# Two block transposes of a staged Fourier mixing, moved from VectorE to DMAs through DRAM

## The chip, the cores and the metric

The kernel runs on one core of one Trainium2 chip. The metric is the device time in microseconds. Where a time comes from the profile, it is from one profiled execution, and its span runs from the first to the last instruction.

## What is computed

The input x has 8 batches of 3008 rows with 256 columns. Along the rows a real Fourier transform is taken, multiplied by a complex filter, and transformed back; the result, 24,064 rows of 256, goes through a two-layer network with a leaky ReLU.

```python
X = np.fft.rfft(x, axis=1)
F = (filt_r + 1j * filt_i)[None, :, :]
y = np.fft.irfft(X * F, n=x.shape[1], axis=1)
h = y.reshape(24064, 256) @ w_in        # 256 x 2048
out = np.maximum(0.01 * h, h) @ w_out   # 2048 x 256
```

## The kernel before

**The transform.** 3008 is split as 94 x 32, so that each direction is two stages of small matrix products with a transpose between them. For one batch the steps are these:

- *s1* (`s1_group`, 16 groups, matmul on L175): a 94-point transform of two of the 32 residues n, with the n-th slices of `x_sb` as moving data. The result has 128 partitions: four quadrants of 32 (real and imaginary parts of two sets of 24 frequencies k, the rest padding). A copy from PSUM writes it to the buffer `big[(4b) % 3]` (`spread`, L185).
- *t1* (`t1_part`, four parts, L197): VectorE transposes 32 x 32 blocks, which exchanges k on the partitions with n along the row, in each quadrant. It goes from one `big` buffer to the next.
- *s2* (`s2_group`, 12 groups, L215): the 32-point transform with the twiddle factors, two frequencies k a group, each with its own weights in `f2_sb`. VectorE then multiplies by the filters into `p1` and `p2` (L220 to L222), and GpSimd adds them to `y` (L224).
- *sa* (`sa_group`, 12 groups, L231): the inverse 32-point transform of y, copied by ACT to a `big` buffer, again by `spread`.
- *t2* (`t2_part`, four parts, L205): the second block transpose.
- *sb* (`sb_group`, 16 groups, L243): the inverse 94-point transform, whose weights are slices of the transposed data; VectorE copies the result to `yt` (L246), which holds two batches.

Batch 0 goes through other functions (`first_s1` to `first_sb`) before the network starts; it uses `t1_part` too, and `first_t2`. In what follows "b" is batches 1 to 7.

**The network.** It runs in 47 chunks of 512 rows. A chunk has 8 slots. In a slot `moe1_group` does a part of the first layer (four matmuls of 512 columns, L380, and an activation on ACT to `gt`, L385), and `moe2_slice` a part of the second layer of the chunk before (eight matmuls of 256 columns, L394). Every second slot ends with a copy to an output staging buffer `ost` on ACT (L401), and every fourth with a store to DRAM on SyncE (L405). There are six staging buffers.

**What sets the order.** All work is written in a fixed order (`tc.manual_schedule()`). The table `tasks` says which transform groups stand in which slot; `plan` fills it. In a slot come first the network's first part, then the transform groups in the order in which they were entered, then the second part:

```python
if ci < NCHUNK:
    moe1_group(ci, g)
for f in tasks.get(slot, ()):
    f()
if ci > 0:
    moe2_slice(ci - 1, g)
```

Batch b has to be in `yt` by slot 47b. With z = 47(b-1) - 8 for b from 2 on, s1 takes two groups a slot from z, t1 stands at z+9 to z+12, s2 from z+13 with a step of 1.25 slots (`(step * g) // 4` with step 5), sa three slots after its s2, t2 at z+32 to z+35 and sb, two groups a slot, from z+37. Batch 1 has the same stages in slots 0 to 39, with one s2 group a slot. The s1 copies of batch 1 go three times in four to VectorE, all others to ACT.

**The x load.** `x_sb` holds one batch. In the slot of the last s1 group of batch b, `x_load(b + 1)` (L136) is put on GpSimd's queue; it converts from float32 and waits for the last matmul that reads `x_sb`. GpSimd also flips a sign in `fb_sb` once (L362), before batch 1.

**PSUM.** s1, s2, sa and sb take turns on three one-bank tiles `pf`, the first layer on two two-bank tiles `ph`, the second layer on `po_ps`.

Of the kernel before, what the change touches and what calls it, by code (L numbers as in the profile page):

```python
# [10 lines left out]
P = 128  # L11
FP16 = mybir.dt.float16
FP32 = mybir.dt.float32
# [5 lines left out]
N1, N2 = 94, 32  # L19
NC = 24  # L20
Q = 32
# [48 lines left out]
def kernel(  # L70
# [9 lines left out]
    nc = tc.nc  # L80
    B, N, D = x.shape
# [16 lines left out]
    f2_sb = cpool.tile([P, NC, P], FP16, name="f2_sb")  # L98
    i1_sb = cpool.tile([P, N2, N1], FP16, name="i1_sb")
# [6 lines left out]
    big = [cpool.tile([P, Q * D], FP16, name=f"big{i}") for i in range(3)]  # L106
    yt = cpool.tile([P, NDT, 2 * N], FP16, name="yt")

    gtp = ctx.enter_context(tc.tile_pool(name="gtp", bufs=2))
    scrp = ctx.enter_context(tc.tile_pool(name="scr", bufs=2))  # L110
    ypp = ctx.enter_context(tc.tile_pool(name="ypp", bufs=4))
    outp = ctx.enter_context(tc.tile_pool(name="outst", bufs=6))
# [8 lines left out]
    def bank(kind, n, w):  # L121
        of = wide if kind == "ph" else single
        t = of[turn[kind] % len(of)]
        turn[kind] += 1
        return t[:, : n * w].rearrange("p (n w) -> p n w", n=n)
# [7 lines left out]
    def x_load(b, n0=0, nn=N2, d0=0, dn=D):  # L133

        for lo, cnt in ((0, R1),) if b + 1 < B else ((0, 64), (64, N1 - 64)):
            nc.gpsimd.dma_start(  # L136
                x_sb[lo : lo + cnt, ds(n0, nn), ds(d0, dn)],
                bass.AP(tensor=x.tensor, offset=x.offset + (b * N + lo * N2 + n0) * D + d0,
                        ap=[[N2 * D, cnt], [D, nn], [1, dn]]))
# [29 lines left out]
    nc.vector.memset(big[2][:].rearrange("p (e n t) -> p e n t", n=Q, t=2)[:, :, NC:Q, :], 0.0)  # L169


    def s1_group(b, g, copy=nc.scalar.copy):
        def go():
            ps = bank("pf", 2, D)
            nc.tensor.matmul(ps, fwd1[:N1], x_sb[:N1, ds(2 * g, 2), :], start=True, stop=True)  # L175
            spread(big[(4 * b) % 3], 2 * g, ps, copy)
        return go


    def paired(t):  # L180
        return t[:].rearrange("p (e n t) -> p n e t", n=Q, t=2)

    def spread(dst, n0, ps, copy, e0=0):
        nn, de = ps.shape[1], ps.shape[2] // 2
        copy(paired(dst)[:, ds(n0, nn), ds(e0, de)], ps.rearrange("p n (e t) -> p n e t", t=2))  # L185

    E4 = D // 2 // 4

    def t1_part(b, i, flat=False):
        def go():  # L190
            a = big[(4 * b) % 3][:].bitcast(FP32)[:, ts(i, E4 * Q)].rearrange("p (e n) -> p e n", n=Q)
            o = big[(4 * b + 1) % 3][:].bitcast(FP32)
            if flat:
                o = o[:, ts(i, E4 * Q)].rearrange("p (e n) -> p e n", n=Q)
            else:
                o = o.rearrange("p (n e) -> p e n", n=Q)[:, ts(i, E4), :]
            nc.vector.transpose(o, a)  # L197
        return go


    def t2_part(b, i):
        def go():
            a = big[(4 * b + 2) % 3][:].bitcast(FP32)[:, ts(i, E4 * Q)].rearrange("p (e n) -> p e n", n=Q)
            o = big[(4 * b + 3) % 3][:].bitcast(FP32).rearrange("p (h n e) -> p h e n", h=2, n=Q)
            nc.vector.transpose(o[:, i // 2, ts(i % 2, E4), :], a)  # L205
        return go

    ys = {}

    def s2_group(b, g):  # L210
        def go():
            ps = bank("pf", 2, D)
            src = big[(4 * b + 1) % 3][:].rearrange("p (n d) -> p n d", n=Q)
            for j in range(2):
                nc.tensor.matmul(ps[:, j, :], f2_sb[:, 2 * g + j, :], src[:, 2 * g + j, :],  # L215
                                 start=True, stop=True)
            fa, fb = fa_sb[:, ds(2 * g, 2), :], fb_sb[:, ds(2 * g, 2), :]
            p1 = scrp.tile([P, 2, D], FP32, tag="p1", name=f"p1_b{b}_g{g}")
            p2 = scrp.tile([P, 2, D], FP32, tag="p2", name=f"p2_b{b}_g{g}")
            nc.vector.tensor_tensor(p1[:], ps, fa, AL.mult)  # L220
            nc.vector.tensor_tensor(p2[0:64], ps[64:P], fb[64:P], AL.mult)  # L221
            nc.vector.tensor_tensor(p2[64:P], ps[0:64], fb[0:64], AL.mult)  # L222
            y1 = ypp.tile([P, 2, D], FP16, tag="y", name=f"y_b{b}_g{g}")
            nc.gpsimd.tensor_tensor(y1[:], p1[:], p2[:], AL.add)  # L224
            ys[(b, g)] = y1
        return go

    def sa_group(b, g):
        def go():
            ps = bank("pf", 2, D)  # L230
            nc.tensor.matmul(ps, inv2, ys.pop((b, g))[:], start=True, stop=True)  # L231
            spread(big[(4 * b + 2) % 3], 2 * g, ps, nc.scalar.copy)
        return go

    def sb_group(b, g, copy):
        dt, h = g // 8, g % 8

        def go():
            src = big[(4 * b + 3) % 3][:].rearrange("p (h n d) -> p h n d", h=2, n=Q)
            ps = bank("pf", 4, N1)  # L240
            for j in range(4):
                n2 = 4 * h + j
                nc.tensor.matmul(ps[:, j, :], src[:, dt, n2, :], i1_sb[:, n2, :],  # L243
                                 start=True, stop=True)
            yv = yt[:, dt, ds((b % 2) * N, N)].rearrange("p (a c) -> p a c", c=N2)
            copy(yv[:, :, ds(4 * h, 4)], ps.rearrange("p c a -> p a c"))  # L246
        return go
# [3 lines left out]
    act, dve = nc.scalar.copy, nc.vector.tensor_copy  # L251
# [70 lines left out]
    g = 0  # L322
    for (n0, nn), fill in zip(first_parts, (4, 3, 1, 14)):
        while nn:
            n = 2 if nn % 4 or n0 >= N2 - 4 else 4
            first_s1(n0, n, two[n // 4], (dve, act)[g % 2])
            n0, nn, g = n0 + n, nn - n, g + 1
# [32 lines left out]
        first_sb(g, act if g in (10, 12, 14) else dve, two[(g // 2) % 2])  # L360

    nc.gpsimd.tensor_scalar(fb_sb[64:P], fb_sb[64:P], -1.0, None, AL.mult)  # L362


    gts, pos, osts = {}, {}, {}
# [43 lines left out]
    tasks = {}  # L409

    def at(slot, f):
        tasks.setdefault(slot, []).append(f)

    def plan(b, s1, per, t1, s2, step, lag, t2, sb):
        for g in range(16):
            at(s1 + g // per, s1_group(b, g, dve if b == 1 and g % 4 < 3 else act))
        if b + 1 < B:
            at(s1 + 15 // per, lambda: x_load(b + 1))
        for i in range(4):
            at(t1 + i, t1_part(b, i))  # L420
        for g in range(12):
            at(s2 + (step * g) // 4, s2_group(b, g))
            at(s2 + lag + (step * g) // 4, sa_group(b, g))
        for i in range(4):
            at(t2 + i, t2_part(b, i))
        for g in range(16):
            at(sb + g // 2, sb_group(b, g, dve))

    plan(1, 0, 2, 8, 13, 4, 3, 27, 32)
    for b in range(2, B):  # L430
        z = 47 * (b - 1) - 8
        plan(b, z, 2, z + 9, z + 13, 5, 3, z + 32, z + 37)

    for slot in range(SL * (NCHUNK + 1)):
        ci, g = divmod(slot, SL)
# [36 lines left out]
```

## Time and profile before

| | |
|---|---|
| median of 3 runs | 780.17 us (780.16 to 780.19) |
| span of the profiled execution | 777.8 us |
| time outside that span, against the median | 2.4 us |
| mean granted clock of TensorE | 0.998 |
| first-layer matmuls (L380) | 386.5 us busy |
| second-layer matmuls (L394) | 381.5 us busy |
| s1 matmuls (L175) | 112, 33.6 us |
| s2 matmuls (L215) | 168, 32.1 us |
| sa matmuls (L231) | 84, 31.8 us |
| sb matmuls (L243) | 448, 28.7 us |
| ACT, activations (L385) | 384.9 us |
| ACT, copies of s1 and sa (L185) | 106.6 us, 605 ns each |
| DVE, copies of sb to yt (L246) | 56.3 us, 544 ns each |
| POOL, sign flip (L362) | 15.7 us, once |
| DMA, mean of the span | 56 GB/s |

How to read it: matmuls are pipelined, and the profile models their ends, so the busy times of neighbouring matmuls overlap; what a group of matmuls holds of TensorE is seen from the distance of one start to the next. "Idle before" in the profile's groups is time in which an engine stood before such an instruction, with the one that released it.

### The profile page before, as it was taken

To read this page: it belongs to the slowest core of one execution; us is meant where nothing else is said; L and a number is where in the kernel's file an instruction comes from. 1 tells how busy PE (TensorE), PEld (TensorE's weight loads), DVE (VectorE), ACT (ScalarE), POOL (GpSimd) and SP (SyncE) were. 2 spreads that over 40 slices of the span, in tenths; PEclk is the share of its full clock that TensorE was granted. 3 is DMA by queue.
4 is the path that set the end of the run, shared out by engine and by line. 5 is a ranking of instruction groups with operands and counts; after the bars stand their busy time and mean duration, and the time that the engine had idled before them with its cause. 6 is when DMAs were issued, how large, how long until landed. Compare 5 with 4: busy or idle time off the path is not lost.

```text
span 777.8 us, 13325 instructions
## 1 busy us (share of the span) xinstructions
PE 768.4 (99%) x5685; PEld 521.3 (67%) x5685; DVE 368.4 (47%) x464; ACT 553.7 (71%) x785; POOL 149.9 (19%) x123
## 2 busy tenths in 40 slices
PE   8899999999999999999999999999999999999998
PEld 4556666667676676666777667666667666766666
DVE  5979743764148741676407743187423765200000
ACT  4877768676787768777586775967668676666664
POOL 4955200330005200151002400025000330000000
PEclk9999999999999999999999999999999999999999
DMA  9961013110151010500105010230101000110111
GB/s 188 220 105 47 28 41 81 56 42 29 41 109 41 28 41 28 120 31 29 41 28 122 28 41 29 53 96 28 41 28 42 28 35 34 42 38 31 41 41 55
DMA packets 36282, 43.36 MB, mean 56 GB/s; under 512 B 8130, under 2 KB 34370, under 8 KB 35458
## 3 DMA queue, kind: packets, MB, share of 16 engines
q0 software_dynamic: 10048, 16.48, 12.3%
q1 hardware_dynamic: 26176, 26.04, 9.5%
q8 instruction: 44, 0.72, 0.4%
q14 instruction: 14, 0.11, 0.0%
HBM read 34.10 MB, written 24.64 MB: 76 GB/s over the span
## 4 chain that ended last, share of the span: by engine, by line
PE 95%; DVE 1%; ACT 1%; DMA 1%; issue 0%; POOL 0%; DVEq 0%; POOLq 0%
PE ph L380 41%; PE po_ps L394 41%; PE pf L175 3%; PE pf L243 2%; PE pf L215 2%; PE pf L231 2%; DMA x_sb<-in_x_dram 1%; PE pf L394 1%; PE pf L290 1%; PE ph L269 1%; ACT big L185 1%; DVE big L197 0%; DVE big L298 0%; DVE prod L283 0%; ACT big L291 0%
## 5 line engine op out<-in xcount | busy, mean ns | idle before, releaser
L385 ACT ACTIVATE gt_c<-ph 128x1024 f16<-128x1024 f32 x376 | 384.9, 1024 | 195.6 <-PE ph L380 193.7
L380 PE MATMUL ph<-yt,w_in_sb 128*128 128x512 f16 (+3 forms) x1600 | 386.5, 366 | 0.3 <-DVE yt L310 0.3
L394 PE MATMUL po_ps<-w_out_sb,gt_c 128*128 128x256 f16 x2944 | 381.5, 272 | 0.5 <-ACT ost_c_t L401 0.5
L394 PEld LDWEIGHTS <-gt_c 128*128 128x128 f16 x3008 | 290.5, 98 | 82.3 <-issue 2.4
L380 PEld LDWEIGHTS <-w_in_sb 128*128 128x128 f16 x1600 | 154.3, 98 | 97.6 <-issue 0.6
L224 POOL TENSOR_TENSOR y_b_g<-p_b_g,p_b_g 128x512 f16<-128x512 f32 x84 | 106.8, 1272 | 225.7 <-DVE p_b_g L222 225.7
L197 DVE STREAM_TRANSPOSE big<-big 128x1024 f32<-128x1024 f32 x32 | 55.9, 1843 | 126.0 <-ACT big L185 125.9
L185 ACT CAST big<-pf 128x512 f16<-128x512 f32 x186 | 106.6, 605 | 1.1 <-PE pf L256 1.1
L246 DVE CAST yt<-pf 128x376 f16<-128x376 f32 x112 | 56.3, 544 | 86.1 <-PE pf L243 86.1
L220 DVE TENSOR_TENSOR p_b_g<-pf,fa_sb 128x512 f32<-128x512 f32 x84 | 58.1, 692 | 38.4 <-PE pf L215 35.5
L401 ACT COPY ost_c_t<-po_ps 128x256 f32<-128x256 f32 x184 | 69.4, 377 | 6.6 <-PE po_ps L394 5.4
L205 DVE STREAM_TRANSPOSE big<-big 128x1024 f32<-128x1024 f32 x28 | 51.0, 1932 | 33.9 <-ACT big L185 33.9
L221 DVE TENSOR_TENSOR p_b_g<-pf,fb_sb 64x512 f32<-64x512 f32 x84 | 58.2, 692 | 1.1
L222 DVE TENSOR_TENSOR p_b_g<-pf,fb_sb 64x512 f32<-64x512 f32 x84 | 57.4, 683 | 1.1
L136 POOL DMA_DIRECT2D x_sb<-in_x_dram x13 | 7.1, 549 | 251.9 <-PE pf L175 251.1
L243 PEld LDWEIGHTS <-big 128*128 128x128 f16 x448 | 25.7, 98 | 13.2
L175 PE MATMUL pf<-x_sb,small_sb 94*128 94x512 f16 x112 | 33.6, 379 | 0.2 <-DVE yt L246 0.2
L215 PE MATMUL pf<-big,f_sb 128*128 128x256 f16 x168 | 32.1, 273 | 0.0
L231 PE MATMUL pf<-y_b_g,small_sb 128*128 128x512 f16 x84 | 31.8, 379 | 0.0
L215 PEld LDWEIGHTS <-f_sb 128*128 128x128 f16 x168 | 16.4, 98 | 19.7
L243 PE MATMUL pf<-i_sb,big 128*128 128x94 f16 x448 | 28.7, 206 | 0.0
L175 PEld LDWEIGHTS <-small_sb 94*128 94x128 f16 x112 | 10.7, 98 | 10.5
(51 smaller groups left out, 166.3 us busy)
## 6 DMA issues: line engine op xcount, KB each, us to landing
out_dram<-ost_c_t SPq DMA_DIRECT2D x92, 256.0 KB, 2.1
x_sb<-in_x_dram POOLq DMA_DIRECT2D x5, 1536.0 KB, 11.0
x_sb<-in_x_dram POOLq DMA_DIRECT2D x2, 768.0 KB, 8.2
x_sb<-in_x_dram POOLq DMA_DIRECT2D x3, 480.0 KB, 8.2
w_in_sb<-in_moe_w_in_dram POOLq DMA_DIRECT2D x1, 1024.0 KB, 13.5
w_out_sb<-in_moe_w_out_dram POOLq DMA_DIRECT2D x1, 1024.0 KB, 10.6
x_sb<-in_x_dram POOLq DMA_DIRECT2D x1, 1024.0 KB, 8.2
fa_sb<-in_filt_r_dram POOLq DMA_DIRECT2D x4, 192.0 KB, 9.6
```

Source lines behind the costliest of these rows:

```text
L175: nc.tensor.matmul(ps, fwd1[:N1], x_sb[:N1, ds(2 * g, 2), :], start=True, stop=True)
L185: copy(paired(dst)[:, ds(n0, nn), ds(e0, de)], ps.rearrange("p n (e t) -> p n e t", t=2))
L215: nc.tensor.matmul(ps[:, j, :], f2_sb[:, 2 * g + j, :], src[:, 2 * g + j, :], start=True, stop=True)
L220: nc.vector.tensor_tensor(p1[:], ps, fa, AL.mult)
L221: nc.vector.tensor_tensor(p2[0:64], ps[64:P], fb[64:P], AL.mult)
L222: nc.vector.tensor_tensor(p2[64:P], ps[0:64], fb[0:64], AL.mult)
L224: nc.gpsimd.tensor_tensor(y1[:], p1[:], p2[:], AL.add)
L243: nc.tensor.matmul(ps[:, j, :], src[:, dt, n2, :], i1_sb[:, n2, :], start=True, stop=True)
L380: nc.tensor.matmul(ph[:, j, ds(o, ln)], w_in_sb[:, dt, ts(ct, P)], yt[:, dt, ds(lo, ln)], start=(dt == 0), stop=(dt == NDT - 1),)
L385: nc.scalar.activation(gts[ci][:, ds(2 * g, 2), :], ph, AF.Lrelu)
L394: nc.tensor.matmul(po, gts[ci][:, ct, ts(tj, P)], w_out_sb[:, ct, :], start=(ct == 0), stop=(ct == NCT - 1))
L401: nc.scalar.copy(ost[:, tj % 2, :], po)
```

## The change

A pool in DRAM gets four scratch tensors, two (`dz1`) for the first transpose and two (`dz2`) for the second, used by batches in turn. For batches 1 to 7 the VectorE transposes are left out. The copies of s1 and sa now write plain rows to a ring of four staging tiles (`st1` and `st2`, halves of `big[2]`), and after every second group SyncE stores such a tile, 128 partitions of 2 KB, to DRAM. Loads on SyncE bring the data back transposed, in runs of 512 bytes: four DMAs, one a quadrant, for four frequencies k (`t1_load`, to a ring of four tiles `z1`), and four DMAs for four residues n (`t2_load`, to the ring `z2`); both rings are halves of `big[1]`. GpSimd sets the half with z2 to zero once, after the sign flip, since `t2_load` fills 24 of each 32 partitions. sb takes its two column halves dt in turn for each n, not one half after the other.

`plan` is new. Groups now stand in slots by fractions, cut to whole slots. From batch 2 on, with z = 47b, s1 starts at z-74 with 1.5 groups a slot, the x load stands in slot z-64 as the last s1 group does, four t1 loads (16 DMAs) in z-62, s2 from z-60 with a step of 2.5 slots, sa two slots after its s2, four t2 loads (16 DMAs) in z-24, and sb from z-22 with 1.5 groups a slot. The other two t1 loads and four t2 loads stand behind the groups that free their places in the ring. In batch 1, s1 starts at 0 with two groups a slot, the t1 loads stand in slot 9, s2 from slot 11 with a step of one slot, sa two slots after it, the t2 loads in 27 and sb from 29 with two groups a slot.

```diff
+    dz1 = [drp.tile([P, N2, D], FP16, name=f"dz1_{i}") for i in range(2)]
+    dz2 = [drp.tile([P, Q, D], FP16, name=f"dz2_{i}") for i in range(2)]
+    def ring(t, half):
+        v = t[:, ts(half, Q * D // 2)].rearrange("p (r n d) -> p r n d", r=4, n=4)
+        return [v[:, r] for r in range(4)]
+    z1, z2 = ring(big[1], 0), ring(big[1], 1)
+    st1, st2 = ring(big[2], 0), ring(big[2], 1)
...
-            spread(big[(4 * b) % 3], 2 * g, ps, copy)
+            h = g // 2
+            copy(st1[h % 4][:, ds(2 * (g % 2), 2), :], ps)
+            if g % 2:
+                nc.sync.dma_start(dz1[b % 2][:, ds(4 * h, 4), :], st1[h % 4])
...
+    def t1_load(b, c):
+        def go():
+            for q in range(4):
+                nc.sync.dma_start(
+                    z1[c % 4][Q * q : Q * q + Q],
+                    dz1[b % 2][Q * q + 4 * c : Q * q + 4 * c + 4].rearrange("k n d -> n k d"))
+        return go
+    def t2_load(b, h):
+        def go():
+            for q in range(4):
+                nc.sync.dma_start(
+                    z2[h % 4][Q * q : Q * q + NC],
+                    dz2[b % 2][Q * q + 4 * h : Q * q + 4 * h + 4, :NC].rearrange("n k d -> k n d"))
         return go
...
-    def t2_part(b, i):
...
-                nc.tensor.matmul(ps[:, j, :], f2_sb[:, 2 * g + j, :], src[:, 2 * g + j, :],
+                nc.tensor.matmul(ps[:, j, :], f2_sb[:, 2 * g + j, :],
+                                 z1[g // 2 % 4][:, 2 * (g % 2) + j, :],
                                  start=True, stop=True)
...
-            spread(big[(4 * b + 2) % 3], 2 * g, ps, nc.scalar.copy)
+            h = g // 2
+            nc.scalar.copy(st2[h % 4][:, ds(2 * (g % 2), 2), :], ps)
+            if g % 2:
+                nc.sync.dma_start(dz2[b % 2][:, ds(4 * h, 4), :], st2[h % 4])
...
-        dt, h = g // 8, g % 8
+        h, dt = g // 2, g % 2
...
-                nc.tensor.matmul(ps[:, j, :], src[:, dt, n2, :], i1_sb[:, n2, :],
+                nc.tensor.matmul(ps[:, j, :], z2[h % 4][:, j, ts(dt, P)], i1_sb[:, 4 * h + j, :],
...
+    nc.gpsimd.memset(big[1][:, ts(1, Q * D // 2)].bitcast(FP32), 0.0)
...
+        tasks.setdefault(int(slot), []).append(f)
+    def plan(b, s1, per, s2, step, lag, sb, rate):
         for g in range(16):
+            at(s1 + g / per, s1_group(b, g, dve if b == 1 and g % 4 < 3 else act))
         if b + 1 < B:
+            at(s1 + 15 / per, lambda: x_load(b + 1))
+        for c in range(4):
+            at(s2 - 2, t1_load(b, c))
         for g in range(12):
+            at(s2 + step * g, s2_group(b, g))
+            if g % 2 and g < 4:
+                at(s2 + step * g, t1_load(b, 4 + g // 2))
+            at(s2 + lag + step * g, sa_group(b, g))
+        for h in range(4):
+            at(sb - 2, t2_load(b, h))
         for g in range(16):
+            at(sb + g / rate, sb_group(b, g, dve))
+            if g % 2 and g < 8:
+                at(sb + g / rate, t2_load(b, 4 + g // 2))
+    plan(1, 0, 2, 11, 1, 2, 29, 2)
     for b in range(2, B):
-        z = 47 * (b - 1) - 8
-        plan(b, z, 2, z + 9, z + 13, 5, 3, z + 32, z + 37)
+        z = 47 * b
+        plan(b, z - 74, 1.5, z - 60, 2.5, 2, z - 22, 1.5)
```

More of the change, by code (lines that the diff above doesn't have):

```diff
@@ L109 @@
     gtp = ctx.enter_context(tc.tile_pool(name="gtp", bufs=2))
+    drp = ctx.enter_context(tc.tile_pool(name="drp", bufs=1, space=bass.MemoryType.DRAM))
     scrp = ctx.enter_context(tc.tile_pool(name="scr", bufs=2))
@@ L169, with s1_group @@
     nc.vector.memset(big[2][:].rearrange("p (e n t) -> p e n t", n=Q, t=2)[:, :, NC:Q, :], 0.0)
-    def s1_group(b, g, copy=nc.scalar.copy):
+    dz1 = [drp.tile([P, N2, D], FP16, name=f"dz1_{i}") for i in range(2)]
[5 more added lines that the diff above has]
+    st1, st2 = ring(big[2], 0), ring(big[2], 1)
+    def s1_group(b, g, copy):
         def go():
@@ L175, in go @@
             nc.tensor.matmul(ps, fwd1[:N1], x_sb[:N1, ds(2 * g, 2), :], start=True, stop=True)
-            spread(big[(4 * b) % 3], 2 * g, ps, copy)
+            h = g // 2
[9 more added lines that the diff above has]
+                    dz1[b % 2][Q * q + 4 * c : Q * q + 4 * c + 4].rearrange("k n d -> n k d"))
+        return go
+    def t2_load(b, h):
[4 more added lines that the diff above has]
+                    dz2[b % 2][Q * q + 4 * h : Q * q + 4 * h + 4, :NC].rearrange("n k d -> k n d"))
         return go
@@ L198, in t1_part @@
         return go
-    def t2_part(b, i):
[L202 to L206, printed above, removed]
     ys = {}
@@ L212, in go @@
             ps = bank("pf", 2, D)
-            src = big[(4 * b + 1) % 3][:].rearrange("p (n d) -> p n d", n=Q)
             for j in range(2):
-                nc.tensor.matmul(ps[:, j, :], f2_sb[:, 2 * g + j, :], src[:, 2 * g + j, :],
+                nc.tensor.matmul(ps[:, j, :], f2_sb[:, 2 * g + j, :],
+                                 z1[g // 2 % 4][:, 2 * (g % 2) + j, :],
                                  start=True, stop=True)
@@ L231, in go @@
             nc.tensor.matmul(ps, inv2, ys.pop((b, g))[:], start=True, stop=True)
-            spread(big[(4 * b + 2) % 3], 2 * g, ps, nc.scalar.copy)
+            h = g // 2
+            nc.scalar.copy(st2[h % 4][:, ds(2 * (g % 2), 2), :], ps)
+            if g % 2:
+                nc.sync.dma_start(dz2[b % 2][:, ds(4 * h, 4), :], st2[h % 4])
         return go
     def sb_group(b, g, copy):
-        dt, h = g // 8, g % 8
+        h, dt = g // 2, g % 2
         def go():
-            src = big[(4 * b + 3) % 3][:].rearrange("p (h n d) -> p h n d", h=2, n=Q)
             ps = bank("pf", 4, N1)
             for j in range(4):
-                n2 = 4 * h + j
-                nc.tensor.matmul(ps[:, j, :], src[:, dt, n2, :], i1_sb[:, n2, :],
+                nc.tensor.matmul(ps[:, j, :], z2[h % 4][:, j, ts(dt, P)], i1_sb[:, 4 * h + j, :],
                                  start=True, stop=True)
@@ L411, in at @@
     def at(slot, f):
-        tasks.setdefault(slot, []).append(f)
-    def plan(b, s1, per, t1, s2, step, lag, t2, sb):
+        tasks.setdefault(int(slot), []).append(f)
+    def plan(b, s1, per, s2, step, lag, sb, rate):
         for g in range(16):
-            at(s1 + g // per, s1_group(b, g, dve if b == 1 and g % 4 < 3 else act))
+            at(s1 + g / per, s1_group(b, g, dve if b == 1 and g % 4 < 3 else act))
         if b + 1 < B:
-            at(s1 + 15 // per, lambda: x_load(b + 1))
-        for i in range(4):
-            at(t1 + i, t1_part(b, i))
+            at(s1 + 15 / per, lambda: x_load(b + 1))
+        for c in range(4):
+            at(s2 - 2, t1_load(b, c))
         for g in range(12):
[L422 to L425, printed above, removed]
+            at(s2 + step * g, s2_group(b, g))
[4 more added lines that the diff above has]
+            at(sb - 2, t2_load(b, h))
         for g in range(16):
-            at(sb + g // 2, sb_group(b, g, dve))
-    plan(1, 0, 2, 8, 13, 4, 3, 27, 32)
+            at(sb + g / rate, sb_group(b, g, dve))
+            if g % 2 and g < 8:
+                at(sb + g / rate, t2_load(b, 4 + g // 2))
+    plan(1, 0, 2, 11, 1, 2, 29, 2)
     for b in range(2, B):
-        z = 47 * (b - 1) - 8
-        plan(b, z, 2, z + 9, z + 13, 5, 3, z + 32, z + 37)
+        z = 47 * b
+        plan(b, z - 74, 1.5, z - 60, 2.5, 2, z - 22, 1.5)
     for slot in range(SL * (NCHUNK + 1)):
```

## The prediction, made before the changed kernel was run

> **What bounds the kernel now.** I read the page first (busy shares, the chain of work that ended last, groups, DMA issues), then the windows by stage, then the timeline of one s2 group, then single DMAs. From the page:
>
> ```profile
> span 777.8 us, 13325 instructions
> ...
> PE 768.4 (99%) x5685; PEld 521.3 (67%) x5685; DVE 368.4 (47%) x464; ACT 553.7 (71%) x785; POOL 149.9 (19%) x123
> ...
> PE 95%; DVE 1%; ACT 1%; DMA 1%; issue 0%; POOL 0%; DVEq 0%; POOLq 0%
> ...
> L197 DVE STREAM_TRANSPOSE big<-big 128x1024 f32<-128x1024 f32 x32 | 55.9, 1843 | 126.0 <-ACT big L185 125.9
> ...
> L205 DVE STREAM_TRANSPOSE big<-big 128x1024 f32<-128x1024 f32 x28 | 51.0, 1932 | 33.9 <-ACT big L185 33.9
> ...
> out_dram<-ost_c_t SPq DMA_DIRECT2D x92, 256.0 KB, 2.1
> x_sb<-in_x_dram POOLq DMA_DIRECT2D x5, 1536.0 KB, 11.0
> ```
>
> TensorE is never without work, and the chain is TensorE's. The transposes that go (28 of L197, 28 of L205) are on VectorE, busy for 47%. The windows (TensorE busy, then the other engines, granted clock, DMA share, GB/s) say where TensorE pauses:
>
> ```profile
> 23.20:26.70 3.50, 3.50 (x21) 2.40 (x22) 3.44 (x4) 1.76 (x4) 3.50 (x4) 0.51 1.05 251
> ...
> 200.00:600.00 400.00, 399.47 (x2984) 274.74 (x2983) 194.15 (x244) 297.06 (x430) 63.67 (x53) 1.00 0.18 50
> ```
>
> In the stages that the change touches TensorE idles 0.53 us of 400: VectorE's work is covered there already. In batch 0, after a wait of 2.0 us behind sparse work, the clock was half for 3.5 us.
>
> Two stretches of the timeline (start, duration, engine). The first gives a slot without transform work; the second follows group 4 of batch 3 from its s2 matmuls to its y:
>
> ```profile
> 130.00 1.04 PE L394 MATMUL po_ps<-w_out_sb,gt_c 128*128 128x256 f16 x8
> 130.87 1.03 PE L380 MATMUL ph<-yt,w_in_sb 128*128 128x512 f16 x4
> 131.73 1.04 PE L394 MATMUL po_ps<-w_out_sb,gt_c 128*128 128x256 f16 x8
> ```
> ```profile
> 242.41 0.38 PE L215 MATMUL pf<-big,f_sb 128*128 128x256 f16 x2
> ...
> 242.62 1.04 PE L394 MATMUL po_ps<-w_out_sb,gt_c 128*128 128x256 f16 x8
> ...
> 242.90 0.69 DVE L220 TENSOR_TENSOR p_b_g<-pf,fa_sb 128x512 f32<-128x512 f32 x1 [1.74 <-PE pf L215]
> ...
> 244.31 0.68 DVE L222 TENSOR_TENSOR p_b_g<-pf,fb_sb 64x512 f32<-64x512 f32 x1
> ...
> 245.13 1.27 POOL L224 TENSOR_TENSOR y_b_g<-p_b_g,p_b_g 128x512 f16<-128x512 f32 x1 [2.56 <-DVE p_b_g L222]
> ```
>
> MoE halves start 0.87 us apart, so an empty slot is 1.735 us; two s2 matmuls hold TensorE 0.21, an s1, sa or sb group about 0.22. y is there at 246.40, 3.99 us after the s2 start, with VectorE free. Nothing waits for it today, since sa follows three slots later.
>
> Last, an output store that SyncE issued at 410.2, 1.6 us after the x load of 408.57:
>
> ```profile
> L405 SPq DMA_DIRECT2D out_dram<-ost_c_t x1: 372/372/372, 410.2 to 410.2; - x1
> ...
> DMA to landing us min/median/max: 10.9/10.9/10.9
> ```
>
> The same store takes 2.1 us elsewhere. Four more, issued 2.8, 4.9, 6.3 and 2.8 us after an x load, took 8.5, 6.9, 5.3 and 8.0 us. Counted from the load's issue they landed at 12.5, 11.3, 11.8, 11.6 and 10.8 us, mean 11.6: **whatever SyncE issues in the shadow of an x load lands when the load has ended.**
>
> **What the Trainium skill says.** "DMA: Bandwidth & Descriptors", "Queues, rings and completion order": a DMA engine takes turns between its queues packet by packet. By that a store should slip through an x load; the five landings disagree, and I follow them. The same page, "Issuing engines are not separate DMA queues": DMAs of SyncE and GpSimd end on the same 16 engines; the landings agree. "TensorE: Matmul & The Clock Gate", "What's actually happening": about 3.4 us of idling halves the clock and about 3.4 us of work restores it; here 3.5 us at 0.51 agree with the second.
>
> **What goes.** 56 transposes, 55.9 x 28/32 + 51.0 = 100 us of VectorE, and TensorE waits for none of them: worth the 0.5 us above at most; I take 0. The new copies are of the same sizes (ACT CAST 605 ns), TensorE's matmuls are the same in number and shape: 0. The POOL memset (8 KB a partition; VectorE's of half the size takes 0.9 us) lies behind the 15.7 us sign flip that ends at 49.3 and ahead of the x load of batch 2 at 49.9: 1.8 to 4 us on the POOL queue, which moves that load to about 51.1; it costs TensorE nothing by itself.
>
> **What SyncE gets.** Per batch 8 stores, 24 loads, 6 stores, 32 loads: 70 DMAs, 490 in all beside 99 now, and 6.7 MB. At 0.37 us each, 0.47 with the gap and a semaphore wait between, that is 33 us of a batch's 94. The thickest stretch, from the t2 loads on (32 loads, 6 stores, 2 output stores in 8 slots, some 17 us), needs 40 x 0.47 = 19 us: SyncE ends it 2 us late. Behind a waiting load stand output stores (6 buffers, three chunks of slack) and s1 stores (a ring of 4, needed back 4 to 5 us later than they land): covered. If that cover fails, ACT stops in its order and the MoE's activations with it. The t2 loads: the first four issue about 0.6 us into slot z-24 and land 3 x 0.47 + 2.1 later, at 4.1; sb needs them two slots and 0.87 on, at 5.0: 0, with 0.9 us to spare (ends 0 to 3 us a batch). The later loads have 5 us or more.
>
> **Step 1: sa two slots after s2.** For batches 2 to 7 s2 starts at slots 0, 2, 5, 7, ... and sa of the same group two slots later; the slot between is empty. TensorE reaches sa after 0.21 + 0.87 + 1.735 + 0.87 = 3.69 us. y is there at 4.00, plus about 0.05 until TensorE starts (0.05 in batch 0 from a transpose to its matmul; up to 0.15 possible): **0.36 us of standing per group**, with all MoE matmuls behind it in order. Of 72 groups I drop ten (first two after each long stall of batches 2 to 6, where sb groups or the half clock fill the gap): 62 x 0.36 = 22.3, and 0.3 for the ends of batch 1, whose other slots hold both s2 and sa (4.1 us). **22.6 us.** Ends: 62 x 0.30 = 19 and 72 x 0.45 = 32.
>
> **Step 2: the t1 loads in the shadow of the x load.** The last s1 matmul of batch b releases two things: the x load of b+1 (issued 0.7 us later, as now) and, through ACT, where its 0.6 us copy stands behind a 1.02 us activation, about 1.7 us later the last s1 store. The store is caught: it lands 11.6 us after the x load's issue. All t1 loads read rows that every store wrote, so they wait for it: fourth load issued at 11.7 + 3 x 0.47 = 13.1, landed at +2.1 = 15.2. TensorE arrives at s2 after 0.22 + 0.87 + three slots of 1.735 with 5 sb groups (1.05) + 0.87 + 0.21 = 8.4 from the s1 matmul, which is 7.7 from the load. Stall 7.5 us, batches 3 to 6: 30.0. Batch 2: four t2 loads of batch 1 stand ahead in the queue, 17.1 against 8.2: 8.9. Batch 1: the memset delays the x load, so the store gets through and the loads themselves are caught: x load at 51.1, landing 11.7 later at 62.8; s2 at slot 11, 54.64 + 0.87 = 55.5: 7.3. Batch 7 has no x load: 0. **46.2 us.** Ends: 36 (stores land at 11, loads in 1.7) and 58 (load delayed by the same traffic, two more queued DMAs).
>
> **Step 3: the clock after a stall.** Six stalls over 7 us; 3.4 us at half clock lose 1.7 each: **10.2 us.** Ends 0 and 20 (twice the window).
>
> **The sum.** 777.8 + 22.6 + 46.2 + 10.2 = 856.8 us of span. The median of the runs is 780.17, 2.4 above this span; with that the time is **859.2 us**. Its own band, from the ends with up to 3 us at some t2 loads: 835 to 885. A measurement of this kernel can tell about 0.2% from no change.
>
> **Rivals.** Fair sharing: the queues take turns as the skill says, the last store lands some 3.5 us after its s1 matmul and the loads at 7 to 10 against 8.4. Then 72 x 0.36 = 26 us of step 1 and 0 to 2 us for six batches: 806 to 818, say **812**. For it: the page; against it: five landings of five. Chance 0.14.
>
> SyncE becomes the bound: loads of 512-byte runs issue or land slower than any row here shows, t2 comes 3 to 5 us late in each of seven batches, or the store ring holds ACT up. 859 + 7 x 3 to 5: **880 to 894**. For it: 19 us of issue in 17; against it: 0.9 us to spare and rows of 0.32 to 0.43 us for DMAs of any shape. Chance 0.18.
>
> Not slower: TensorE's order in a slot is not that of the code, so that sa slides behind more MoE matmuls and s2 behind more slots; both waits are then covered, and the time is **780**. It decides from 0.36 us, four L394 matmuls, for sa, and from 7.5 us for s2. Against it: in the timeline L380, L215, L394 stand in the code's order throughout. Chance 0.04.
>
> **How the numbers follow.** The sum above has 0.64. The range 820 to 888 holds all of its band, half of SyncE's case and little of the other two. Only the last case isn't slower: slower 0.96, same 0.03, faster 0.01.
>
> **What would show it.** Step 1: TensorE waits for y (L224) some 60 to 70 times, 0.3 to 0.4 us each; none, and it is wrong. Step 2: six waits of 6 to 10 us at the s2 matmuls for a DMA, before batches 1 to 6 and not 7; stores issued just after an x load landing in about 10 us. Step 3: a clock of about 0.5 for some 3.4 us after each, a mean clock near 0.985. VectorE's busy time near 268 us. The prediction fails if the t1 loads land within 8 us of the last s1 matmul, or if ACT waits for st1 or st2.

## The result, and the profile after

The changed kernel takes 876.52 us (median of 4 runs, 874.2 to 879.92) against 780.18 us before: ratio 1.1238, 95% interval 1.1212 to 1.1264, slower. The prediction was 859.2 us with a range of 820 to 888. The profiled execution took 877.4 us, with a span of 875.6 us, 97.8 us more than before.

From the page of the changed kernel, the lines that answer to those of before; the last three are groups, with the idle time of TensorE ahead of them and what ended it:

```profile
span 875.6 us, 14160 instructions
...
PE 795.4 (91%) x5685; PEld 527.3 (60%) x5685; DVE 268.1 (31%) x408; ACT 554.8 (63%) x785; POOL 151.2 (17%) x124
...
PE 55%; DVE 19%; DMA 10%; POOL 10%; issue 3%; SPq 2%; ACT 1%; DVEq 0%; POOLq 0%
...
L267 PE MATMUL pf<-i_sb,big 128*128 128x94 f16 x448 | 32.8, 211 | 28.9 <-DMA big<-dz 28.9
...
L237 PE MATMUL pf<-big,f_sb 128*128 128x256 f16 x168 | 33.5, 283 | 25.5 <-DMA big<-dz 25.2
...
L254 PE MATMUL pf<-y_b_g,small_sb 128*128 128x512 f16 x84 | 31.6, 377 | 15.1 <-POOL y_b_g L247 15.1
```

VectorE lost 100 us of work, as it should, and the chain that ends last now runs through VectorE, GpSimd and DMAs for some 40%. TensorE stands before sb (L267) and s2 (L237) for a load from `dz`, and before sa (L254) for y. The waits on SyncE's queue show where the loads stand:

```profile
SPq L196 <- DMA dz<-big: 45.2, 6, 10.9
```

Six times, up to 10.9 us, the first t1 load (L196) waits for the last s1 store. One of the six, batch 3, in the timeline (start, duration, engine):

```profile
224.46 0.53 POOL L137 DMA_DIRECT2D x_sb<-in_x_dram  x1 [30.36 <-PE pf L186]
...
225.57 1.92 SPq L204 DMA_DIRECT2D big<-dz  x4
...
227.59 0.38 SPq L190 DMA_DIRECT2D dz<-big  x1
...
237.50 0.47 PE L267 MATMUL pf<-i_sb,big 128*128 128x94 f16 x4 [5.53 <-DMA big<-dz]
...
238.03 7.42 SPq L196 DMA_DIRECT2D big<-dz  x16
...
241.31 0.58 PE L237 MATMUL pf<-big,f_sb 128*128 128x256 f16 x2 [3.34 <-DMA big<-dz]
```

The x load of the next batch is issued at 224.46. What SyncE issues after it is caught: four t2 loads of batch 2 (225.57), on which an sb group waits until 237.50, and the last s1 store (227.59), after whose landing the t1 loads start at 238.03. s2 begins at 241.31, 9.2 us late. The windows over the same stretch (TensorE busy, the other engines, granted clock, DMA share, GB/s):

```profile
232.00:241.30 9.30, 0.47 (x4) 0.31 (x5) 0.55 (x1) 1.02 (x1) 0.00 (x0) 0.78 0.55 141
241.30:244.10 2.80, 2.79 (x12) 1.74 (x13) 2.07 (x3) 0.37 (x1) 0.00 (x0) 0.50 0.49 139
```

After the stall TensorE works 2.8 us at half clock.

How a DMA is caught stands in the trace's records of single packets, the pieces in which the 16 DMA engines move data. The x load has 96 packets of 16 KB, 1.23 us long or longer: six an engine on average. Ahead of the loads and the store named above, SyncE's queue holds an output store, whose issue at 223.86 lasted until after the x load's; it has 256 packets of 1 KB and 0.06 us, 16 an engine, and landed at 236.6. From 227 to 229 us 25 packets of the x load start and none of SyncE's; from 230 to 232 us 29 of each. From 229 to 235 us every packet of SyncE's that starts is the output store's. So the two queues take turns, one packet for one, but a turn of the load takes 1.23 us or more: with six such turns an engine, most of the output store is still left when the load ends, and with it all that stands behind it in SyncE's queue.

**Where the 97.8 us are.** I took the starts of all matmuls from 40 us on, subtracted from each distance what the first of the two holds TensorE (0.2165 us for 512 columns, 0.1085 for 256, 0.0445 for 94), booked the doubled time at half clock apart, and gave the rest to the matmul that came late. The work itself is 731 us before and 732 after.

| term | predicted | measured |
|---|---|---|
| late at sa (step 1) | 22.6 | 26.0, 67 times 0.39 |
| late at sb and s2 for a DMA (step 2) | 46.2 | 56.6 |
| half clock (step 3) | 10.2 | 13.7 |
| everything else | 0 | 1.5 |

Step 2 by batch, 1 to 6: 8.2, 10.8, 9.2, 9.6, 8.1, 10.0 us; batch 7, which has no x load, 0.

### The profile page after: what moved, and what is told of

It reads as the page before. It is cut to its first block, busy times and chain, and to the rows that moved or that the text cites. A ratio compares the mean times of both kernels' runs of the same rounds, so it can differ in the third digit from the quotient of the medians.

```text
span 875.6 us, 14160 instructions
## 1 busy us (share of the span) xinstructions
PE 795.4 (91%) x5685; PEld 527.3 (60%) x5685; DVE 268.1 (31%) x408; ACT 554.8 (63%) x785; POOL 151.2 (17%) x124
## 4 chain that ended last, share of the span: by engine, by line
PE 55%; DVE 19%; DMA 10%; POOL 10%; issue 3%; SPq 2%; ACT 1%; DVEq 0%; POOLq 0%
PE ph L405 22%; PE po_ps L419 21%; POOL y_b_g L247 9%; DMA dz<-big 7%; DVE p_b_g L245 6%; DVE p_b_g L244 6%; DVE p_b_g L243 6%; PE pf L254 3%; PE pf L186 3%; PE pf L237 2%; DMA big<-dz 2%; PE pf L267 2%; SPq L204 1%; DMA x_sb<-in_x_dram 1%; SPq L196 1%
## 5 line engine op out<-in xcount | busy, mean ns | idle before, releaser
L405 PE MATMUL ph<-yt,w_in_sb 128*128 128x512 f16 (+3 forms) x1600 | 390.7, 369 | 0.3 <-DVE yt L334 0.3
L419 PE MATMUL po_ps<-w_out_sb,gt_c 128*128 128x256 f16 x2944 | 389.0, 276 | 0.0
L419 PEld LDWEIGHTS <-gt_c 128*128 128x128 f16 x3008 | 295.2, 99 | 103.0 <-issue 21.3
L267 PE MATMUL pf<-i_sb,big 128*128 128x94 f16 x448 | 32.8, 211 | 28.9 <-DMA big<-dz 28.9
L267 PEld LDWEIGHTS <-big 128*128 128x128 f16 x448 | 28.2, 101 | 48.5 <-DMA big<-dz 24.7
L237 PE MATMUL pf<-big,f_sb 128*128 128x256 f16 x168 | 33.5, 283 | 25.5 <-DMA big<-dz 25.2
L188 ACT CAST big<-pf 128x512 f16<-128x512 f32 x100 | 55.6, 589 | 0.0
L237 PEld LDWEIGHTS <-f_sb 128*128 128x128 f16 x168 | 15.9, 98 | 56.1 <-issue 31.8
L256 ACT CAST big<-pf 128x512 f16<-128x512 f32 x84 | 48.7, 580 | 0.0
L254 PE MATMUL pf<-y_b_g,small_sb 128*128 128x512 f16 x84 | 31.6, 377 | 15.1 <-POOL y_b_g L247 15.1
L186 PE MATMUL pf<-x_sb,small_sb 94*128 94x512 f16 x112 | 36.7, 379 | 1.4 <-ACT big L256 1.3
L386 POOL TENSOR_SCALAR fb_sb<-fb_sb 64x6144 f16<-64x6144 f16 x1 | 15.7, 15737 | 0.1
L186 PEld LDWEIGHTS <-small_sb 94*128 94x128 f16 x112 | 10.4, 98 | 8.0 <-issue 0.3
## 6 DMA issues: line engine op xcount, KB each, us to landing
w_in_sb<-in_moe_w_in_dram POOLq DMA_DIRECT2D x1, 1024.0 KB, 13.6
```

Source lines behind the costliest of these rows:

```text
L237: nc.tensor.matmul(ps[:, j, :], f2_sb[:, 2 * g + j, :], z1[g // 2 % 4][:, 2 * (g % 2) + j, :], start=True, stop=True)
L267: nc.tensor.matmul(ps[:, j, :], z2[h % 4][:, j, ts(dt, P)], i1_sb[:, 4 * h + j, :], start=True, stop=True)
L405: nc.tensor.matmul(ph[:, j, ds(o, ln)], w_in_sb[:, dt, ts(ct, P)], yt[:, dt, ds(lo, ln)], start=(dt == 0), stop=(dt == NDT - 1),)
L419: nc.tensor.matmul(po, gts[ci][:, ct, ts(tj, P)], w_out_sb[:, ct, :], start=(ct == 0), stop=(ct == NCT - 1))
```

## The experiments

All are edits of the changed kernel, runs 6 to 8 on top of an earlier run's; every ratio is to the kernel before, run on the same chip.

**1. The x load later.** In the program it stands two slots after s2 begins.

```diff
-            at(s1 + 15 / per, lambda: x_load(b + 1))
+            at(s2 + 2, lambda: x_load(b + 1))
```

> The x load of the next batch is issued two slots after s2 begins instead of with the last s1 group; nothing else changes. Theory A (SyncE's DMAs stand in the shadow of the x load, and TensorE waits for them at sb and s2, then runs at half clock): the DMA waits of TensorE, 56 us in the changed kernel, fall below 5 us, the half clock after them, 14 us, goes with them, the sa waits of 26 us stay or rise by 2 to 4 us since no long stall covers the first ones: 876.5 - 56 - 14 + 3 = about 809 us. Theory B (SyncE's own queue of 490 DMAs is the bound, the x load only happens to stand there): the waits stay at 30 us or more, time 850 us or more.

Measured: 819.1 us, ratio 1.0493 (1.0477 to 1.0509). TensorE's waits of that kernel:

```profile
PE pf L254 <- POOL y_b_g L247: 14.9, 67, 0.6
PE pf L237 <- DMA big<-dz: 8.9, 6, 4.0
```

The wait at sb is gone, the one at s2 is 10.5 us by the sum of starts, not under 5; half clock 1.4 us. 57 us of the change's cost hang on when the x load is issued. Theory A's 809 us are missed by 10: what stays at s2, 4.1 us of it in batch 2, was not in its number.

**2. A lag of three slots.** sa three slots after its s2.

```diff
-    plan(1, 0, 2, 11, 1, 2, 29, 2)
+    plan(1, 0, 2, 11, 1, 3, 29, 2)
-        plan(b, z - 74, 1.5, z - 60, 2.5, 2, z - 22, 1.5)
+        plan(b, z - 74, 1.5, z - 60, 2.5, 3, z - 22, 1.5)
```

> sa stands three slots after its s2 instead of two, in all batches; nothing else changes. Theory A (y is ready 4.0 us after s2 begins, two slots give 3.7 us, three give 5.4): the waits of TensorE for y, 26 us, vanish, the DMA waits stay: about 850 us. Rival (TensorE only waits elsewhere, the rate of VectorE and GpSimd or of SyncE sets the pace): 870 us or more.

Measured: 853.0 us, ratio 1.0934 (1.0908 to 1.096). In TensorE's waits the line of y is gone, the DMA lines stay:

```profile
PE pf L267 <- DMA big<-dz: 28.1, 5, 8.4
PE pf L237 <- DMA big<-dz: 26.5, 6, 9.3
```

23.5 us by the lag alone, as theory A has it: step 1 is a matter of the plan, not of the DMAs.

**3. Both.** The edits of 1 and 2 together.

> Late x load and a lag of three slots together. Theory A: both kinds of wait are independent of one another and gone, TensorE is busy throughout as in the kernel before: 780 to 786 us. Rival (490 DMAs on SyncE, or the copies through DRAM, cost TensorE something of their own, for instance at the t2 loads): 795 us or more.

Measured: 794.6 us, ratio 1.0186 (1.0171 to 1.0202): between theory A's number and its rival's, and 0.4 us from the rival's. The two terms add up (57 + 23.5 taken from 876.5 is 796), but 14 us stay. By the starts, 10.3 are at s2 groups, mostly the first of a batch (2.5 in batch 1, 4.3 in batch 2, about 1 in each of three others), and 2.4 half clock. In batch 2 the trace shows SyncE issuing t2 loads of batch 1 until 111.4; the t1 loads start only then, and s2 follows at 115.28, 4.3 us late. So the first t1 loads are late even without an x load, by what stands ahead of them in SyncE's queue. Whether that is a latency or a rate, runs 5 to 7 were to tell.

**4. The s1 stores on ACT's queue.**

```diff
-                nc.sync.dma_start(dz1[b % 2][:, ds(4 * h, 4), :], st1[h % 4])
+                nc.scalar.dma_start(dz1[b % 2][:, ds(4 * h, 4), :], st1[h % 4])
```

> The eight s1 stores of a batch are issued on ACT's queue, behind ACT's own copies, instead of on SyncE's; all else as in the changed kernel. In the changed kernel the last s1 store of batch 3 is issued 3.8 us after its matmul, since four t2 loads and an output store stand ahead of it, and lands 13.6 us after the x load's issue. Theory A (the store is caught in the shadow in any case, SyncE's backlog only adds some 2 us a batch): the store lands about 11.5 us after the x load's issue, the waits shrink by 1.5 to 2.5 us in each of batches 2 to 6: 862 to 870 us. Rival (the backlog is what puts the store into the shadow; without it the store gets through): waits at s2 vanish except those at sb, 845 us or less. A second rival (DMAs issued by ACT delay its activations, 8 x 0.4 us a batch): 876 us or more.

Measured: 880.7 us, ratio 1.1303 (1.1277 to 1.1329), so theory A's time is missed, and the second rival has the time. Theory A and this rival were each half right. In batch 3 the last store is issued 0.9 us after the x load and lands 11.0 us after it (13.6 in the changed kernel): SyncE's backlog did add 2.6 us. The DMA waits of all batches are 50.7 us for 56.6, 1.2 us less a batch in batches 2 to 6, where theory A had 1.5 to 2.5. The packets show why a store that goes ahead of the backlog, on a queue of its own, is caught all the same: it has 128 packets of 2 KB, eight an engine, and from 233 to 237 us 47 packets of the x load, 39 of the store and 31 of SyncE's t2 loads start, in turns. But TensorE now waits for ACT elsewhere:

```profile
PE po_ps L419 <- ACT ost_c_t L426: 3.9, 10, 0.5
```

By the starts the network's matmuls come 8.0 us later in all than in the changed kernel: I put that down to the eight stores a batch, 0.33 us each, which stand in line with ACT's copies and activations.

**5. The x load in short runs**, even and odd residues n in two DMAs, 512 bytes a run in SBUF instead of 16 KB.

```diff
+    def x_rows(b):
+        for lo, cnt in ((0, R1),) if b + 1 < B else ((0, 64), (64, N1 - 64)):
+            for odd in range(2):
+                nc.gpsimd.dma_start(
+                    x_sb[lo : lo + cnt, odd::2, :],
+                    bass.AP(tensor=x.tensor, offset=x.offset + (b * N + lo * N2 + odd) * D,
+                            ap=[[N2 * D, cnt], [2 * D, N2 // 2], [1, D]]))
...
-            at(s1 + 15 / per, lambda: x_load(b + 1))
+            at(s1 + 15 / per, lambda: x_rows(b + 1))
```

> The x load stands where the changed kernel has it, but as two DMAs, of the even and of the odd residues n, so that it moves in runs of 512 bytes in SBUF and not 16 KB; the same bytes. Theory T (the DMA engines take turns between the queues packet by packet, so that an 8-packet store only had to wait for 16 KB packets of 1.2 us each): with small packets SyncE's DMAs get through, stores issued in the shadow land within 5 us, TensorE's DMA waits fall from 56 us to below 25 and the half clock goes: 835 us or less. Theory F (what is queued for the x load is drained before SyncE's DMAs, whatever the packets): the last s1 store still lands with the end of the load, 10 us or more after it was issued, and the load takes as long or longer: 870 us or more.

Measured: 872.7 us, ratio 1.1181 (1.1162 to 1.12): theory F's time. The DMA waits are 51.4 us by the starts, not below theory T's 25; part of them moves from sb to s2:

```profile
PE pf L245 <- DMA big<-dz: 41.4, 6, 8.4
...
PE pf L275 <- DMA big<-dz: 8.2, 3, 3.9
```

In batch 4 the two loads are issued at 331.07 and 332.05 and land at 341.8 and 346.5. The s1 store, issued at 332.81 behind both, lands at 341.2, with the end of the first; the t1 loads, issued while the second still runs, land in 3 to 5 us instead of 1.9. But theory F's reason isn't what the packets show. While the first load runs, from 333 to 339 us, 468 packets of SyncE's start to 1198 of the loads; the store's come last of these, behind t2 loads and the 256 packets of an output store issued at 332.31. So short runs let SyncE's DMAs in, and the store still took 8.4 us. Ahead of the t1 loads SyncE's queue had been empty; whether that is why they fared better is open.

**6. s2 two slots later, the x load with it** (from run 3's kernel; the x load kept its slot number, but in that slot it now stands ahead of the first y, which made this another test than the one meant).

```diff
-            at(s2 + 2, lambda: x_load(b + 1))
+            at(s2, lambda: x_load(b + 1))
-            at(s2 - 2, t1_load(b, c))
+            at(s2 - 4, t1_load(b, c))
-    plan(1, 0, 2, 11, 1, 3, 29, 2)
+    plan(1, 0, 2, 13, 1, 3, 31, 2)
-        plan(b, z - 74, 1.5, z - 60, 2.5, 3, z - 22, 1.5)
+        plan(b, z - 74, 1.5, z - 58, 2.5, 3, z - 22, 1.5)
```

> Late x load and lag of three slots as in the kernel of 794.6 us, and s2 and sa stand two slots later while the t1 loads stay where they are (in batch 1 the t2 loads and sb also go two slots later). What is left in that kernel are waits of 1 to 4 us at the first s2 group of a batch, 10 us in all, and 2.4 us of half clock. Theory A (the first four t1 loads come late by SyncE's queue ahead of them, a latency and not a rate): two slots, 3.5 to 3.9 us a batch, cover them: 780 to 784 us. Rival (SyncE's 490 DMAs are a rate that TensorE meets somewhere, so the waits move to later groups): 790 us or more.

Measured: 835.2 us, ratio 1.0699 (1.0675 to 1.0723). Theory A's number is missed; the rival's is met, but not for its reason: the waits were back at sb (32.4 us by the starts), with an early x load. GpSimd's timeline says why, here first of run 6's kernel and then of run 1's:

```profile
220.12 0.53 POOL L137 DMA_DIRECT2D x_sb<-in_x_dram  x1 [26.71 <-PE pf L186]
241.62 1.27 POOL L247 TENSOR_TENSOR y_b_g<-p_b_g,p_b_g 128x512 f16<-128x512 f32 x1 [20.98 <-DVE p_b_g L245]
```
```profile
217.85 1.27 POOL L247 TENSOR_TENSOR y_b_g<-p_b_g,p_b_g 128x512 f16<-128x512 f32 x1 [41.03 <-DVE p_b_g L245]
219.05 0.53 POOL L137 DMA_DIRECT2D x_sb<-in_x_dram  x1
```

A slot is no time: on GpSimd only its own queue and the semaphores count. Entered ahead of the first y of its batch, the load waits for nothing but the last s1 matmul and goes out with it, as in the changed kernel; entered behind that y, it goes out after it. Two slots for s2 took 17 us off the DMA waits of run 2, which has the same early load.

**7. The x load behind the first y** (from run 6's kernel).

```diff
-            at(s2, lambda: x_load(b + 1))
+            at(s2 + 1, lambda: x_load(b + 1))
-            at(s2 - 4, t1_load(b, c))
+            at(s1 + 18 / per, t1_load(b, c))
-    plan(1, 0, 2, 13, 1, 3, 31, 2)
+    plan(1, 0, 2, 12, 1, 3, 30, 2)
```

> As the kernel of 835.2 us, with the x load put one slot after the first s2 group. There it stood in GpSimd's queue ahead of that group's y, with nothing before it to wait for but the last s1 matmul, so it was issued with the last s1 group again; here the y of group 0 stands ahead of it. In batch 1, s2 and sb stand one slot later than in the changed kernel, not two. Theory A (the shadow of the x load is a matter of when GpSimd reaches it, and the rest of 14 us in the kernel of 794.6 us is the lateness of the first t1 loads): DMA waits of TensorE below 3 us in all, 781 to 786 us. Rival (SyncE's DMAs are a rate that TensorE meets somewhere): 792 us or more.

Measured: 799.4 us, ratio 1.0251 (1.0236 to 1.0266), which the numbers give to the rival; the trace doesn't. Of the 19 us left, 13.4 are one wait and 1.5 the half clock around it:

```profile
117.75 0.43 SPq L196 DMA_DIRECT2D big<-dz  x1
118.28 1.76 SPq L204 DMA_DIRECT2D big<-dz  x4
118.54 0.53 POOL L137 DMA_DIRECT2D x_sb<-in_x_dram  x1
...
129.93 0.78 PE L267 MATMUL pf<-i_sb,big 128*128 128x94 f16 x8 [13.20 <-DMA big<-dz]
```

The last four t2 loads of batch 1 stand behind the t1 loads of batch 2. By their semaphores the first of them, issued at 118.28, 0.26 us before the x load, landed in 2.20 us; the second, issued at 118.67, 0.13 us after it, in 10.75. Again in turns: from 121 to 128 us 80 packets of the x load start and 69 of SyncE's. A t2 load has 96 packets and, by its semaphore, 12 of the 16 engines: eight each on average, against the x load's six.

**8. Batch 1's s2 and sb back in their slots** (from run 7's kernel).

```diff
-    plan(1, 0, 2, 12, 1, 3, 30, 2)
+    plan(1, 0, 2, 11, 1, 3, 29, 2)
```

> As the kernel of 799.4 us, with batch 1's s2 and sb where the changed kernel has them (slots 11 and 29). In the kernel of 799.4 us one wait of 13.4 us was left: the last t2 loads of batch 1 stood behind the 16 t1 loads of batch 2 in SyncE's queue, and three of the four were issued just after the x load. One slot earlier they stand ahead of the t1 loads. Theory A (order in SyncE's queue against the moment of the x load): that wait goes, about 2 us come back at the first s2 of batch 1: 784 to 789 us. Rival (SyncE's DMAs are a rate): a wait of that size turns up elsewhere, 795 us or more.

Measured: 786.2 us, ratio 1.0092 (1.0076 to 1.0107), as theory A has it: 0.8 to 1.1% slower than the kernel before. With all 490 DMAs in place, TensorE has no pause from 200 to 600 us:

```profile
200.00:600.00 400.00, 400.00 (x2987) 274.84 (x2985) 144.53 (x227) 290.71 (x416) 67.12 (x57) 1.00 0.42 124
```

The rest against the kernel before is 4.4 us at s2 groups, nearly all of batch 1, and 2.3 us of single late matmuls. So the DMAs as a rate cost nothing there, and VectorE's 100 us bring nothing: a kernel whose TensorE is never without work has no use for them. No version beat the kernel before.

## Why the prediction was right, and where its sizes were off

- **What goes is worth nothing**: right. Run 8 has no transposes, no wait over 0.2 us after the first 86 us, and isn't faster.
- **Step 1**: right. Predicted 62 waits of 0.36 us, measured 67 of 0.39; run 2 takes them out and gets 23.5 us. I dropped ten groups as covered, and only half of those were.
- **Step 2**: the mechanism was right (runs 1, 2 and 8, and batch 7 without a wait), the term was 10.4 us too small. The failing piece is in "What SyncE gets": I worked out that SyncE ends its thickest stretch 2 us late and called it covered, and "the later loads have 5 us or more". Those 2 us put the last t2 loads of the batch before and the last s1 store behind the x load. In batch 3 the store was issued 3.8 us after its matmul, not 1.7, and landed 13.6 us after the x load's issue, not 11.6; the t1 loads landed 3.2 us after that, against 3.6 predicted. Run 4 shows the piece by itself: without the backlog the store lands at 11.0, and the DMA waits are 5.9 us shorter; part of that may be TensorE coming later there, so the piece's share of the 10.4 us isn't shown exactly. It also moved part of the wait: I expected all six at s2, and in batches 2 to 6 the longer part, 5 to 7.5 us, is at an sb group of the batch before, which waits for a caught t2 load. TensorE would have waited for the same x load a little later anyway.
- **Step 3**: right in kind. The clock was at half for 6.8 to 10.2 us around each stall, of which I had counted the last 3.4; most of that lies in the stall itself and costs nothing. Measured by the starts it cost 13.7 us, 2.3 a stall, for 1.7 predicted.
- **The rivals**: fair sharing is out as a time (the first t1 loads landed at 241.2 in batch 3, 17.4 us after the last s1 matmul, not 7 to 10), but the turns it rests on are there, and my reading that the five landings disagree with them was wrong. In the kernel before, too, from 415 to 418 us 33 packets of the x load and 32 of the output store issued at 410.18 start. What failed was the step from turns to "slips through": a turn of the x load costs 1.23 us or more, and a DMA of 8 to 16 packets an engine needs more turns than the load has packets. My rule that what is caught lands when the load has ended held by this count, not against the turns. SyncE as the bound is out as a rate (run 8), but as a latency it is in the result: in part of the 10 us too few of step 2 (run 4), and in 8 of the 14 us that run 3 kept. TensorE kept the code's order in every stretch looked at.
- **The band**: its upper end, 885 us, doesn't follow from the ends given. 780.2 + 32 + 58 + 20 is 890, without the 3 us at some t2 loads; the measured 876.5 lies inside either.
- What stays open: why none of SyncE's packets start in the first stretch beside a load (227 to 229 us in the changed kernel; in the kernel before the store issued at 410.18 has its first packet at 414.2), and why the turns were not one for one with the short packets of run 5. A load of another length wasn't tried, and neither were DMAs of fewer packets on SyncE.

## What to carry to other kernels

Before work is moved to DMAs, ask what else the DMA engines hold at that moment: here each transfer took about 2 us by itself and 10 to 12 us if a 1.5 MB load of 16 KB packets had been issued just before. Count the packets: each one that a DMA engine has of the transfer waits for a packet of the load, 1.23 us or more here, until the load is through. And the load is released by the very matmul that the transfer follows. Put such a load behind an instruction on its own queue that ends where the load may start; its place in a plan of slots doesn't hold it back. And a lag between producer and consumer is to be counted in microseconds of the slots as they will be: two slots of 1.735 us are no cover for 4.0 us.

## What the runs showed of the hardware that I had not expected

- Turns between queues, one packet for one, don't protect a small transfer: 29 packets of 1 KB to 29 of 16 KB in 2 us, and three queues in turn in run 4 (47, 39 and 31 packets in 4 us).
- How sharp the edge of a load's shadow is: of two DMAs of 48 KB on one queue, 0.39 us apart, with an x load between them, one took 2.20 us and the next 10.75.
- Cutting the load's runs from 16 KB to 512 bytes let SyncE's packets run beside it (468 to 1198 in 6 us), yet a store of 256 KB queued behind others still took 8.4 us.
- The GpSimd memset of 128 x 2048 float32 took 1.80 us, the low end of what I had allowed.
